# Subtracting the maximum in both softmaxes of a two-way attention read ahead of a gated FFN

## The chip, the core and the metric

One core of a Trainium2 chip runs the kernel. The metric is the device time of one execution in microseconds (us). TensorE is called PE (its weight loads PEld), VectorE DVE, ScalarE ACT, GpSimd POOL, and the sync engine, which issues most DMAs, SP.

## What is computed

```python
B, H, S, Ns, D = 8, 8, 512, 32, 64           # x: (B,H,S,D), state: (B,H,Ns,D)
scores = x @ state.T / sqrt(D)                # per batch and head, S x Ns
a = exp(scores - scores.max(-1)); a /= a.sum(-1) + 1e-9
xread = a @ state
scores2 = state @ x.T / sqrt(D)               # Ns x S
a2 = exp(scores2 - scores2.max(-1)); a2 /= a2.sum(-1) + 1e-9
sread = a2 @ x
y = concat([xread, sread], axis=2)            # heads side by side: (B*544, 512)
out = (sigmoid(y @ w_gate) * (y @ w_val)) @ w_out     # 512 -> 1536 -> 512
```

The first softmax runs over the 32 states of a token ("over states"), the second over the 512 tokens of a state ("over tokens"). Inputs and output are float32; matmuls take bfloat16.

## The kernel before

A batch is one of the eight values of B. Its 512 tokens are handled in four chunks c (token 4p + c on partition p), its 8 heads in four pairs j (e is the head within a pair).

- `load_x`, `cast_x` (L70, L88) bring x of a batch into `xf` and cast it to `xb`. `xT`, with head pairs on the partitions, comes by PE transposes for batches 0 and 1 (`xT_mm`, `xT_cp`) and by DMA transposes on SP from batch 2 on (`at_xT_dma`, L110).
- `S_mm(b, i)` (L115) makes the scores of half the head pairs in one PSUM bank, `S_exp` (L123) takes the exponential from PSUM into `E1` with no maximum subtracted. One exponential serves both softmaxes.
- Over states: `n_sum` (L137) sums over states and takes the reciprocal, `n_mul` (L169) multiplies into `ab`; `aT`, its transpose, comes by PE (batches 0 and 1) or by DMA on SP (`aT_dma`, L192).
- Over tokens: `at_Eb` (L129) casts `E1` to bfloat16 on POOL; `n_tok` and `n_split` (L143, L161; `p_tok` on POOL for batch 1) add the four chunks and split the sum into two bfloat16 terms; `sr_mm` (L201) multiplies a matrix of ones with them (L210: column sums) and `xb` with `Eb` (L213); `sr_inv` and `sr_fin` (L216, L220) divide and put the result into `XS`.
- The read over states is never formed: `sw_visit` and `sw_wide` (L239, L255) make state times w_gate and w_val for a batch in PSUM by 64x32 matmuls (L236), `sw_cp` copies it to `SW`. `gv_mm(b, f)` (L280) then makes gate and value of 128 of the 1536 channels from `SW` and `aT`: four matmuls of 128x128 by 512. `gv_th` (ACT, tanh for the sigmoid) and `gv_glu` (DVE) give `glu`. `out_mm(b, k)` (L310) makes a third of an output chunk with four matmuls; every third call ends in `res` on ACT (L323) and a DMA on SP. A ninth pass, b = 8, does the FFN of all state rows from `XS`.

Each engine runs its instructions in the order in which the code issues them; nothing is reordered. Two parts fix that order: a hand-written list from L392 to L652, which loads, brings up batches 0 and 1 and starts batch 2 (the fill), and a loop from L654 on, with twelve slots f per batch: in slot f, `out_mm(b - 1, f)`, then `gv_mm(b, f)` with tanh and glu (slots 0 and 6: `sw_wide` of the next batch first, then gv, then out), and beside it a share of the next batch's attention. `warm` (L349) issues matmuls whose result is not used.

PSUM has eight banks in four pools: `p_gv` (GV, 2), `p_out` (OU, 1), `p_sw` (SWP, 4), `p_at` (AT, 1). `sw_wide` takes all but GV: its first two tiles lie in OU and AT. A tile's bank is free when its last reader is done.

Of the kernel before, what the change touches and what calls it, by code (L numbers as in the profile page):

```python
# [16 lines left out]
def kernel(  # L17
# [70 lines left out]
    def cast_x(b, cp, lo, n):  # L88
        if b not in xbs:
            xbs[b] = xp.tile((128, 4, H, D), BF, name="xb")  # L90
        cp(xbs[b].rearrange("p c h d -> p h c d")[:, lo:lo + n], xfs[b][:, lo:lo + n])  # L91
# [31 lines left out]
    def S_exp(b, i):  # L123
        if b not in E1s:
            E1s[b] = ap_.tile((128, 4, 2, 4, Ns), FP, name="E1")
        nc.scalar.activation(E1s[b][:, :, :, 2 * i:2 * i + 2].rearrange("p c e j n -> p (c e) j n"),  # L126
                             held["S", b, i].rearrange("p c e j n -> p (c e) j n"), AF.Exp, scale=scale)

    def at_Eb(b):  # L129
        Ebs[b] = ap_.tile((128, 4, 2, 4, Ns), BF, name="Eb")  # L130
        for c in range(4):
            nc.gpsimd.tensor_copy(Ebs[b][:, c], E1s[b][:, c])  # L132
# [9 lines left out]

    def n_tok(b, e):  # L143

        if e == 0:
            held["E4", b] = ap_.tile((128, 2, 4, Ns), FP, name="E4")
        nc.vector.tensor_reduce(held["E4", b][:, e].rearrange("p j n -> p (j n)"),  # L147
                                E1s[b][:, :, e].rearrange("p c j n -> p (j n) c"), AX.X, ALU.add)

    def p_tok(b):  # L150

        E4, E5 = (ap_.tile((128, 2, 4, Ns), FP, name=f"P{i}", bufs=1) for i in range(2))
        add = nc.gpsimd.tensor_tensor
        add(E4, E1s[b][:, 0], E1s[b][:, 1], ALU.add)
        add(E5, E1s[b][:, 2], E1s[b][:, 3], ALU.add)
        add(E4, E4, E5, ALU.add)
        Es[b] = ap_.tile((128, 2, 2, 4, Ns), BF, name="Es")
        pool(Es[b][:, 0], E4)
        add(Es[b][:, 1], E4, Es[b][:, 0], ALU.subtract)

    def n_split(b, k):  # L161

        if k == 0:
            Es[b] = ap_.tile((128, 2, 2, 4, Ns), BF, name="Es")
            nc.vector.tensor_copy(Es[b][:, 0], held["E4", b])
        else:
            nc.vector.tensor_tensor(Es[b][:, 1], held["E4", b], Es[b][:, 0], ALU.subtract)
# [28 lines left out]
    def sr_parts(b):  # L196
        ps = held["sr", b]
        return (ps[:, 0:256].rearrange("p (j e n) -> p j e n", j=4, e=2),
                ps[:, 256:384].rearrange("p (j n) -> p j n", j=4))

    def sr_mm(b, place):  # L201
        Eb = Ebs[b]
        held["sr", b] = place[0].tile((128, 512), FP, name="srp", tag=place[1])
        sr, sm = sr_parts(b)
        if b in Es:
            terms = [(e, Es[b][:, k, e]) for e in range(2) for k in range(2)]
        else:
            terms = [(e, Eb[:, c, e]) for e in range(2) for c in range(4)]
        for i, (e, rhs) in enumerate(terms):
            nc.tensor.matmul(sm, ones[:, e], rhs, start=(i == 0), stop=(i == len(terms) - 1))  # L210
        for j in range(4):
            for c in range(4):
                nc.tensor.matmul(sr[:, j], xbs[b][:, c, 2 * j:2 * j + 2].rearrange("p h d -> p (h d)"),  # L213
                                 Eb[:, c, :, j], start=(c == 0), stop=(c == 3))

    def sr_inv(b):  # L216
        r2 = held["r2", b] = ap_.tile((128, 4, Ns), FP, name="r2")
        nc.vector.reciprocal(r2, sr_parts(b)[1])  # L218

    def sr_fin(b):  # L220
        if ("r2", b) not in held:
            sr_inv(b)
        sr, r2 = sr_parts(b)[0], held["r2", b]
        for e in range(2):
            rows = slice(e * 64, (e + 1) * 64)
            nc.vector.tensor_tensor(XS[rows, :, b * Ns:(b + 1) * Ns], sr[rows, :, e], r2[rows], ALU.mult)
# [166 lines left out]
    load_x(0, nc.sync, 4)  # L393
    load_x(1, nc.sync, 4)
# [4 lines left out]
    nc.vector.memset(sTz, 0.0)  # L399
    ident_e = ident.rearrange("p (g e u) -> p e g u", e=2, u=8)  # L400
    pre = wp.tile((128, 2), FP, name="pre")
    nc.scalar.activation(pre[:, 0:1], ones[:, 0, 0:1], AF.Exp)

    cast_x(0, pool, 0, 2)
    warm(12, OU)
    cast_x(0, vec, 2, 2)
    warm(16, GV)
    warm(8, OU)
    cast_s(0, pool)
    load_w(1, 256, 256)  # L410
# [24 lines left out]
    load_w(1, 0, 256)
    cast_x(1, act, 0, 2)
    S_mm(0, 0, AT, (1,))
    S_exp(0, 1)
    cast_x(1, vec, 4, 2)
    n_sum(0, 1)  # L440
    load_w(0, 512, 512)
    S_exp(0, 0)
    xT_mm(1, 0, SWP)
    xT_mm(1, 1, SWP)
    cast_x(1, pool, 6, 2)
    at_Eb(0)
    xT_mm(1, 2, AT)
    xT_cp(1, 2, vec)
    n_sum(0, 0)
    xT_mm(1, 3, OU)  # L450
    xT_cp(1, 3, act)
    S_mm(1, 1, GV)
    load_sb(2)
    xT_cp(1, 0, act)
    S_exp(1, 1)
    xT_cp(1, 1, vec)
    S_mm(1, 0, AT)
    n_mul(0, 1, nc.vector)
    n_mul(0, 0, nc.vector)
    n_sum(1, 1)  # L460
    sw_visit(0, 256, 256)
    sr_mm(0, OU)
    S_exp(1, 0)
    sw_cp(0, 256, 2, 1, act)
    aT_mm(0, AT)
    sw_visit(1, 256, 256)
    sw_cp(0, 256, 2, 0, act)
    aT_cp(0, 0, act)
    n_sum(1, 0)
    sw_visit(1, 0, 256)  # L470
    aT_cp(0, 1, vec)
    load_w(0, 1024, 512)
    load_w(1, 512, 512)
    load_w(1, 1024, 512)
    n_mul(1, 1, nc.gpsimd)
    sr_fin(0)
# [72 lines left out]
    sw_cp(1, 1024, 1, 0, vec)
    gv_glu(1, 1)  # L550
    cast_x(2, act, 0, 4)
    cast_x(2, pool, 4, 4)
    sw_visit(0, 512, 512, 1)
    gv_mm(1, 11, SWP)
    gv_glu(1, 6)
    sw_cp(0, 512, 1, 0, vec)
    gv_mm(0, 11, GV)
    gv_th(1, 11)
    sw_cp(0, 512, 1, 1, vec)
    at_xT_dma(2)  # L560
    gv_glu(1, 11)
    gv_mm(0, 6, SWP)
    gv_mm(0, 9, SWP)
    gv_th(0, 11)
    gv_th(0, 6)
    gv_glu(0, 11)
    gv_mm(0, 10, GV)
    gv_glu(0, 6)
    gv_th(0, 9)
    gv_mm(0, 7, SWP)  # L570
    gv_glu(0, 9)
    gv_mm(0, 5, SWP)
    gv_th(0, 10)
    gv_th(0, 7)
    gv_th(0, 5)
    load_wo(1)
    gv_glu(0, 7)
    gv_glu(0, 10)
    gv_mm(1, 4, SWP)
    gv_th(1, 4)  # L580
    gv_glu(0, 5)
    gv_mm(0, 4, GV)
    gv_mm(1, 8, SWP)
    gv_glu(1, 4)
    gv_mm(0, 8, SWP)
    sr_fin(1)
    gv_th(1, 8)
    pad(2, 6)
    out_mm(0, 0, AT)
    gate(glus[1][:, 4, 0:1])  # L590
    load_wo(2)
    load_x(3, nc.gpsimd)
    gv_th(0, 4)
    gv_mm(1, 9, SWP)
    gv_th(0, 8)
    gv_glu(1, 8)
# [141 lines left out]
```

## Time and profile before

| | |
|---|---|
| Time, median of 3 runs | 225.48 us (225.43 to 225.87) |
| The profiled execution | 226.03 us, of which the span of its instructions is 224.2 us |
| PE, DVE, ACT, POOL busy | 217.0, 140.7, 127.6, 48.8 us |
| First gate matmul (L288) starts | 16.40 us |
| First `sw_wide` of the loop starts | 56.22 us |
| One steady batch of the loop | 23.6 us |
| DMA | 27.37 MB, mean 122 GB/s |

Times in the profile count from the span's start. A row of the timeline gives start, duration, engine, line and operation, output<-input with partitions x elements, the count where several are merged, and in brackets how long the engine was idle before and what ended that. A PE duration includes the time to drain, so the step to the next matmul is shorter than it. The chain of work is followed back from the last instruction to whatever released each one.

### The profile page before, as it was taken

The page shows a single profiled execution, that of the slowest core. Times are in us where ns is not written, and L with a number is a line of the kernel's source. Part 1 is how long each engine was busy: PE and PEld are TensorE (multiplying, and loading weights), DVE is VectorE, ACT ScalarE, POOL GpSimd, SP SyncE. Part 2 cuts the span into 40 slices and gives each one's busy share as a digit, 9 for nine tenths or more (in the row PEclk, how much of TensorE's full clock was granted, in tenths as well). Part 3 has the DMA queues.
Part 4 walks back from the last instruction along what each step waited for, and adds up shares of the span by engine and source line. Part 5 has one row for each costly group of instructions (what it writes and reads, how often), then busy time and mean ns, then how long its engine had stood idle before and what let it go on. Part 6 is the DMA issues. An engine that isn't in the chain of part 4 may idle for free.

```text
span 224.2 us, 4791 instructions
## 1 busy us (share of the span) xinstructions
PE 217.0 (97%) x1859; PEld 111.2 (50%) x1859; DVE 140.7 (63%) x248; ACT 127.6 (57%) x239; POOL 48.8 (22%) x85
## 2 busy tenths in 40 slices
PE   7789999999999999999999999999999999999994
PEld 6654444444444545454444454454445444466744
DVE  3599897779368756885488648864787434422311
ACT  2587885645676557656675667556755444423311
POOL 3799560362041004200240006000200000000001
PEclk9999999999999999999999999999999999999999
DMA  6999989753898352627362521253122111111114
GB/s 188 289 201 206 280 130 179 114 193 78 147 292 274 71 151 76 219 59 126 100 225 50 121 96 61 44 81 117 47 78 66 50 50 47 67 73 48 50 26 114
DMA packets 38566, 27.37 MB, mean 122 GB/s; under 512 B 21168, under 2 KB 33840, under 8 KB 38544
## 3 DMA queue, kind: packets, MB, share of 16 engines
q1 hardware_dynamic: 31392, 19.74, 32.5%
q0 software_dynamic: 6864, 7.14, 17.6%
q8 instruction: 14, 0.23, 0.4%
q10 hardware_dynamic: 288, 0.20, 0.3%
q14 instruction: 8, 0.07, 0.1%
HBM read 18.35 MB, written 8.91 MB: 122 GB/s over the span
## 4 chain that ended last, share of the span: by engine, by line
PE 91%; DVE 3%; DMA 2%; ACT 1%; SPq 1%; issue 0%
PE outp L319 38%; PE gvp L288 37%; PE swp L236 5%; PE gvp L291 5%; DMA xf<-in_x_dram 2%; PE srp L213 1%; PE Sp L121 1%; PE outp L339 1%; DVE rs L139 1%; PE srp L210 1%; SPq L74 1%; DVE ab L173 1%; DVE ri L141 0%; DVE r L218 0%; PE xTp L105 0%; PE warm L353 0%
## 5 line engine op out<-in xcount | busy, mean ns | idle before, releaser
L303 DVE SCALAR_TENSOR_TENSOR glu<-th,gvp 128x512 bf16<-128x512 f32 (+1 forms) x108 | 69.9, 655 | 64.0 <-ACT th L298 48.7
L319 PE MATMUL outp<-wo,glu 128*128 128x512 bf16 x396 | 98.2, 379 | 0.0
L288 PE MATMUL gvp<-aT,SW 128*128 128x512 bf16 x384 | 96.3, 379 | 0.3 <-DVE aT L190 0.2
L298 ACT ACTIVATE th<-gvp 128x512 f32<-128x512 f32 (+1 forms) x108 | 61.8, 574 | 60.6 <-PE gvp L288 49.2
L288 PEld LDWEIGHTS <-SW 128*128 128x128 bf16 x384 | 36.3, 98 | 44.7 <-issue 3.1
L319 PEld LDWEIGHTS <-glu 128*128 128x128 bf16 x396 | 37.4, 98 | 40.8 <-issue 0.4
L274 ACT CAST SW<-swp 128x512 bf16<-128x512 f32 x70 | 38.8, 586 | 4.7 <-PE swp L236 3.3
L132 POOL CAST Eb<-E 128x256 bf16<-128x256 f32 x32 | 11.5, 407 | 89.9 <-ACT E L126 89.9
L323 ACT ACTIVATE res<-outp 128x512 f32<-128x512 f32 x33 | 19.7, 597 | 17.6 <-PE outp L319 17.6
L274 DVE CAST SW<-swp 128x512 bf16<-128x512 f32 x26 | 17.1, 683 | 1.6 <-PE swp L236 1.4
L91 POOL CAST xb<-xf 128x1024 bf16<-128x1024 f32 (+1 forms) x13 | 13.8, 1093 | 12.1 <-DMA xf<-in_x_dram 10.7
L330 POOL DMA_DIRECT2D out_dram<-res x2 | 1.1, 542 | 60.0 <-ACT res L323 60.0
L147 DVE TENSOR_REDUCE E<-E 128x128 f32<-128x512 f32 x12 | 12.4, 1035 | 0.0
L139 DVE TENSOR_REDUCE rs<-E 128x16 f32<-128x512 f32 x16 | 10.8, 676 | 1.3 <-ACT E L126 1.3
L126 ACT ACTIVATE E<-Sp 128x512 f32<-128x512 f32 x16 | 9.6, 604 | 2.4 <-PE Sp L121 2.4
L173 DVE TENSOR_TENSOR ab<-E,ri 128x512 bf16<-128x512 f32 x12 | 9.6, 804 | 0.0
L236 PE MATMUL swp<-wg,sTc 64*32 64x512 bf16 (+1 forms) x192 | 8.4, 328 | 0.0
L236 PEld LDWEIGHTS <-sTc 64*32 64x32 bf16 x384 | 4.5, 91 | 7.4 <-issue 4.7
L218 DVE RECIPROCAL r<-srp 128x128 f32<-128x128 f32 x8 | 7.6, 950 | 0.0
L121 PEld LDWEIGHTS <-xT 128*128 128x128 bf16 x128 | 5.5, 98 | 4.0 <-DVE xT L108 1.0
L236 PE MATMUL swp<-wv,sTc 64*32 64x512 bf16 (+1 forms) x192 | 7.4, 322 | 0.0
L291 PE MATMUL gvp<-XS,wg 128*128 128x256 bf16 x48 | 7.2, 273 | 0.0
(64 smaller groups left out, 122.0 us busy)
## 6 DMA issues: line engine op xcount, KB each, us to landing
out_dram<-res SPq DMA_DIRECT2D x31, 256.0 KB, 2.6
xf<-in_x_dram SPq DMA_DIRECT2D x12, 256.0 KB, 4.5
xf<-in_x_dram SPq DMA_DIRECT2D x3, 1024.0 KB, 6.8
wo<-in_moe_w_out_dram POOLq DMA_DIRECT2D x3, 512.0 KB, 5.9
wg<-in_moe_w_gate_dram POOLq DMA_DIRECT2D x2, 512.0 KB, 9.2
wv<-in_moe_w_val_dram POOLq DMA_DIRECT2D x2, 512.0 KB, 10.8
xf<-in_x_dram POOLq DMA_DIRECT2D x2, 512.0 KB, 10.4
xf<-in_x_dram POOLq DMA_DIRECT2D x1, 1024.0 KB, 9.2
```

The source lines that it names most:

```text
L91: cp(xbs[b].rearrange("p c h d -> p h c d")[:, lo:lo + n], xfs[b][:, lo:lo + n])
L139: nc.vector.tensor_reduce(rs, halfE(b, i), AX.X, ALU.add)
L147: nc.vector.tensor_reduce(held["E4", b][:, e].rearrange("p j n -> p (j n)"), E1s[b][:, :, e].rearrange("p c j n -> p (j n) c"), AX.X, ALU.add)
L173: eng.tensor_tensor(abs_[b].rearrange("p c e (j n) -> p (c e) j n", n=Ns)[:, ce, 2 * i:2 * i + 2], halfE(b, i)[:, ce], ri[:, ce].unsqueeze ...
L236: nc.tensor.matmul(pss[e][j * Ns:(j + 1) * Ns, o:o + n], sTc[rows, b, j] if b > 1 else sTz[rows, b, j, e], (wg, wv)[w][rows, j, lo:lo + n] ...
L274: cp(*sw_left.pop((b, lo, w, e)))
L288: nc.tensor.matmul(ps, SWs[b][:, g, w, fs], aTs[b][:, :, g], start=(g == 0), stop=(g == 1))
L291: nc.tensor.matmul(ps, (wg, wv)[w][:, j, fs], XS[:, j], start=(j == 0), stop=(j == 3))
L298: nc.scalar.activation(th, held["gv", b, f][0], AF.Tanh, scale=0.5)
L303: nc.vector.scalar_tensor_tensor(glus[b][:, f], held["th", b, f], 1.0, held["gv", b, f][1], ALU.add, ALU.mult)
L319: nc.tensor.matmul(ops[b, c], glus[b][:, f, c * 128:(c + 1) * 128], wo[:, f], start=(f == 0), stop=(f == NF - 1))
L323: nc.scalar.activation(res, ops[b, c], AF.Copy, scale=0.5)
```

## The change

Over states: `S_max` takes the maximum of each token and head over its 32 scores on DVE, from PSUM; `S_sub` subtracts it, PSUM to `E1`; `S_exp` runs in place on `E1`.

Over tokens: `cT_mm` makes the scores once more, transposed (states on the partitions, tokens along the row, 32 states by 4 pairs per bank), `cT_max` their maximum and its scaled negative, `cT_exp` the exponential with that as bias and the sum as a second output, `cT_nrm` the reciprocal (DVE) and the product in bfloat16 (POOL), `c_dma` transposes the two rows back by DMA on SP. `sr_mm` has no sums left, and `sr_cp`, one half on ACT and one on DVE, copies its result. `at_Eb`, `n_tok`, `p_tok`, `n_split`, `sr_inv` and `sr_fin` are gone.

The fill is written anew: batch 1 is loaded and brought up ahead of batch 0, and the transposed scores of batches 0 and 1 are made in the loop's pass of batch 7. `xb` and `xT` of batches 0 and 1 have buffers of their own until then; `xb` of the others has three. In the loop `cast_x` and `at_xT_dma` stand in slot 1 instead of 5, and `n_mul` runs on POOL.

```diff
@@ functions
-    def S_exp(b, i):
-        nc.scalar.activation(E1s[b][...], held["S", b, i], AF.Exp, scale=scale)
+    def S_max(b, i):
+        mx = held["mx", b, i] = ap_.tile((128, 8, 2), FP, name="mx")
+        nc.vector.tensor_reduce(mx, ps, AX.X, ALU.max)
+    def S_sub(b, i):
+        nc.vector.tensor_tensor(halfE(b, i), ps, mx.unsqueeze(3).to_broadcast((128, 8, 2, Ns)), ALU.subtract)
+    def S_exp(b, i):
+        nc.scalar.activation(halfE(b, i), halfE(b, i), AF.Exp, scale=scale)
-    def at_Eb(b): / n_tok / p_tok / n_split / sr_parts / sr_inv / sr_fin
+    def cT_mm(b, places):
+        pss = [p[0].tile((128, 512), FP, name="cTp", tag=p[1]) for p in places]
+        for j in range(4):
+            for e in range(2):
+                rows = slice(e * 64, (e + 1) * 64)
+                nc.tensor.matmul(pss[e][j * Ns:(j + 1) * Ns], sTz[rows, b, j, e],
+                                 xTs[b][rows, j].rearrange("p c t -> p (c t)"), start=True, stop=True)
+    def cT_max(b, e):
+        nc.vector.tensor_reduce(mx, held["cT", b][e], AX.X, ALU.max)
+        nc.vector.tensor_scalar(nb, mx, -scale, None, op0=ALU.mult)
+    def cT_exp(b, e):
+        nc.scalar.activation(ex, held["cT", b][e], AF.Exp, bias=held["nb", b, e], scale=scale, accum_out=cs)
+    def cT_nrm(b, e, eng):
+        nc.vector.reciprocal(rc, held["cs", b, e])
+        eng.tensor_scalar(held["cN", b][:, e], held["cE", b, e], rc, None, op0=ALU.mult)
+    def c_dma(b):
+        for e in range(2):
+            nc.sync.dma_start_transpose(Ebs[b][:, :, e], held["cN", b][:, e])
     def sr_mm(b, place):
-        for i, (e, rhs) in enumerate(terms):
-            nc.tensor.matmul(sm, ones[:, e], rhs, ...)
         for j in range(4):
             for c in range(4):
                 nc.tensor.matmul(sr[:, j], xbs[b][:, c, 2 * j:2 * j + 2]..., Eb[:, c, :, j], ...)
+    def sr_cp(b, e, cp):
+        cp(XS[rows, :, b * Ns:(b + 1) * Ns], held["sr", b][rows, :, e])
@@ the fill, up to the first gate matmul (in part)
+    load_x(1, nc.sync, 4)
...
+    load_x(0, nc.sync, 4)
...
+    cast_x(0, vec, 0, 2)
+    S_mm(1, 0, SWP)
+    xT_cp(1, 2, vec)
+    S_max(1, 0)
...
+    n_sum(1, 1)
...
+    S_max(0, 0)
+    sw_visit(1, 256, 256)
...
+    S_sub(0, 0)
+    S_max(0, 1)
+    S_exp(0, 0)
+    n_mul(1, 1, nc.gpsimd)
+    aT_mm(1, GV)
+    aT_cp(1, 0, act)
...
+    sw_visit(1, 512, 512, 1)
+    S_sub(0, 1)
+    S_exp(0, 1)
+    sw_visit(0, 512, 512, 1)
...
+    warm(15, GV)
...
+    aT_cp(1, 1, vec)
+    gv_mm(1, 3, GV)
@@ the loop, b = 3 to 6 (batch 2 one slot later; nb = b + 1)
+    slot 0: S_mm(nb, 0, AT)
+    slot 1: S_max(nb, 0); S_mm(nb, 1, SWP); cast_x, at_xT_dma of nb + 1
+    slot 2: S_sub(nb, 0); S_max(nb, 1)
+    slot 3: S_exp(nb, 0); S_sub(nb, 1); sr_mm(b, AT)
+    slot 4: sr_cp(b) on act and vec; n_sum, n_mul(nb, 0); S_exp(nb, 1)
+    slot 5: n_sum, n_mul(nb, 1)            slot 6: aT_dma(nb)
+    slot 7: cT_mm(nb, (AT, SWP))           slot 8: cT_max(nb, 0)
+    slot 9: cT_exp(nb, 0); cT_max(nb, 1)   slot 10: cT_exp(nb, 1); cT_nrm(nb, 0)
+    slot 11: cT_nrm(nb, 1); c_dma(nb)
+    b = 7: the same five steps of cT for batch 0 in slots 0 to 4 and for batch 1 in 3 to 7,
+           sr_mm and sr_cp of batch 0 in slot 8 and of batch 1 in slot 11
```

The loop's part is written here as a table of slots; the sw_cp on ACT stay where they were (slots 0, 1, 3, 4 and 6, 7, 9, 10).

More of the change, by code (lines that the diff above doesn't have):

```diff
@@ L194, in aT_dma @@
             nc.sync.dma_start_transpose(aT_tile(b)[:, c], abs_[b][:, c].rearrange("p e k -> p (e k)"))
[L196 to L199, printed above, removed]
-    def sr_mm(b, place):
[L202 to L208, printed above, removed]
-        for i, (e, rhs) in enumerate(terms):
-            nc.tensor.matmul(sm, ones[:, e], rhs, start=(i == 0), stop=(i == len(terms) - 1))
+    def cT_mm(b, places):
[5 more added lines that the diff above has]
+                                 xTs[b][rows, j].rearrange("p c t -> p (c t)"), start=True, stop=True)
+        held["cT", b] = pss
@@ L214, in sr_mm @@
                                  Eb[:, c, :, j], start=(c == 0), stop=(c == 3))
[L216 to L226, printed above, removed]
+    def sr_cp(b, e, cp):
+        rows = slice(e * 64, (e + 1) * 64)
+        cp(XS[rows, :, b * Ns:(b + 1) * Ns], held["sr", b][rows, :, e])
     sw_left = {}
@@ L458 @@
[L458 to L464, printed above, removed]
+    load_x(0, nc.sync, 4)
+    cast_x(1, pool, 0, 2)
+    xT_mm(1, 0, SWP)
+    xT_cp(1, 0, vec)
+    load_w(1, 256, 256)
+    xT_mm(1, 1, AT)
+    load_sb(1)
+    load_w(0, 256, 256)
+    sT_pad(0, 0, act)
+    load_w(1, 512, 512)
+    cast_x(1, act, 4, 2)
+    xT_cp(1, 1, act)
+    xT_mm(1, 2, GV)
+    cast_x(1, pool, 6, 2)
+    cast_x(0, vec, 0, 2)
@@ new lines @@
+    S_mm(1, 0, SWP)
+    xT_cp(1, 2, vec)
+    S_max(1, 0)
+    xT_mm(0, 0, AT)
+    xT_mm(1, 3, SWP)
+    cast_x(0, act, 2, 2)
+    xT_mm(0, 1, GV)
+    xT_cp(0, 0, act)
+    xT_cp(1, 3, act)
+    warm(3, OU)
+    load_w(0, 0, 256)
+    S_sub(1, 0)
+    xT_cp(0, 1, act)
+    cast_x(0, act, 4, 2)
+    S_mm(0, 0, GV, (0,))
+    S_mm(1, 1, SWP)
+    S_exp(1, 0)
+    cast_x(0, vec, 6, 2)
+    warm(3, AT)
+    xT_mm(0, 3, GV)
+    xT_mm(0, 2, SWP)
+    S_max(1, 1)
+    xT_cp(0, 2, act)
+    load_sb(3)
@@ new lines @@
+    load_w(1, 0, 256)
+    warm(6, OU)
+    S_sub(1, 1)
+    load_sb(2)
+    load_w(0, 512, 512)
+    S_mm(0, 0, AT, (1,))
+    warm(12, SWP)
+    n_sum(1, 0)
+    S_exp(1, 1)
+    S_mm(0, 1, AT, (0,))
+    sT_mm(1, SWP)
+    xT_cp(0, 3, act)
+    S_mm(0, 1, OU, (1,))
+    n_mul(1, 0, nc.gpsimd)
+    sw_visit(0, 256, 256)
+    n_sum(1, 1)
+    sT_cp(1, act)
+    sw_cp(0, 256, 2, 0, act)
+    warm(8, GV)
+    S_max(0, 0)
+    sw_visit(1, 256, 256)
+    sw_cp(1, 256, 2, 0, act)
+    sw_cp(0, 256, 2, 1, vec)
@@ new lines @@
+    gv_th(0, 9)
+    gv_glu(0, 9)
+    gv_th(0, 11)
+    gv_th(0, 8)
+    load_wo(2)
+    S_max(2, 0)
+    S_sub(2, 0)
+    S_exp(2, 0)
+    S_mm(2, 1, GV)
+    out_mm(0, 6, AT)
+    load_x(3, nc.gpsimd)
+    cast_x(3, pool, 4, 4)
+    out_mm(0, 2)
+    sw_cp(2, 0, 0, 1, act)
+    gv_glu(0, 8)
+    gv_glu(0, 11)
+    sw_cp(2, 0, 1, 0, act)
+    cT_mm(2, (SWP, SWP))
+    sw_visit(1, 1024, 512, 0)
+    n_sum(2, 0)
+    out_mm(0, 8)
+    n_mul(2, 0, nc.vector)
+    sw_cp(2, 0, 2, 1, act)
+    sw_cp(2, 0, 1, 1, act)
@@ new lines @@
+    S_max(2, 1)
+    S_sub(2, 1)
+    sw_cp(2, 0, 2, 0, act)
+    sw_cp(2, 0, 0, 0, act)
+    S_exp(2, 1)
+    cT_max(2, 0)
+    sw_cp(1, 1024, 0, 0, act)
+    out_mm(0, 7, GV)
+    gate(xTs[2][:, 0, 3, 0:1])
+    cT_max(2, 1)
+    cast_x(3, pool, 0, 4)
+    cT_exp(2, 0)
+    n_sum(2, 1)
+    n_mul(2, 1, nc.vector)
+    aT_dma(2)
+    cT_exp(2, 1)
+    cT_nrm(2, 1, nc.gpsimd)
+    out_mm(0, 10)
+    gv_mm(1, 7, SWP)
+    out_mm(0, 9)
+    gv_th(1, 7)
+    sw_cp(1, 1024, 0, 1, vec)
+    sw_wide(2, 1)
@@ L563 @@
[L563 to L589, printed above, removed]
@@ L654, with row @@
+    def row(b, f):
+        if f == 0:
+            S_mm(b, 0, AT)
+        elif f == 1:
+            S_max(b, 0)
+            S_mm(b, 1, SWP)
+        elif f == 2:
+            S_sub(b, 0)
+            S_max(b, 1)
+        elif f == 3:
+            S_exp(b, 0)
+            S_sub(b, 1)
+        elif f == 4:
+            n_sum(b, 0)
+            n_mul(b, 0, nc.gpsimd)
+            S_exp(b, 1)
+        elif f == 5:
+            n_sum(b, 1)
+            n_mul(b, 1, nc.gpsimd)
     for b in range(2, B + 1):
```

409 lines of the change are left out of this document (166 added, 243 removed).

## Prediction

> **What bounds the kernel now.** I read the first page first: busy time by engine and the span in 40 slices.
>
> ```profile
> PE 217.0 (97%) x1859; PEld 111.2 (50%) x1859; DVE 140.7 (63%) x248; ACT 127.6 (57%) x239; POOL 48.8 (22%) x85
> ...
> PE   7789999999999999999999999999999999999994
> ```
>
> PE is busy in every slice but the first few, so a busy share alone cannot tell a bound from a queue of slow matmuls. The chain of work that ended last can.
>
> ```profile
> PE 91%; DVE 3%; DMA 2%; ACT 1%; SPq 1%; issue 0%
> ```
>
> The chain is PE almost everywhere; DVE, ACT and DMA stand in it only before 18 us. Next the table by stretches. A steady batch takes 23.6 us and PE has no gap in it, while DVE has 7.0 us free and ACT 8.7.
>
> ```profile
> 103.50:127.10 23.60, 23.60 (x197) 11.11 (x196) 16.58 (x27) 14.94 (x29) 3.87 (x6) 1.00 0.49 124
> ```
>
> The columns are the stretch, then busy us of PE, PEld, DVE, ACT and POOL, the granted clock (1.00) and DMA. So the time is the start of the first gate matmul (L288, 16.40 us), plus all PE work behind it, plus waits, and almost none are there today. I price the change in these three terms. The profiled execution took 226.03 us around a span of 224.2; the runs' median is 225.48, so I add the difference in span to 225.48.
>
> **Term 1, PE work.** Three stretches of the timeline give prices (start, us, engine, line).
>
> ```profile
> 22.13 1.04 PE L288 MATMUL gvp<-aT,SW 128*128 128x512 bf16 x4
> ...
> 23.10 0.41 PE L236 MATMUL swp<-wg,sTz 64*32 64x512 bf16 x8
> ...
> 23.44 1.90 PE L288 MATMUL gvp<-aT,SW 128*128 128x512 bf16 x8
> ```
>
> Four gate matmuls step by 0.863 us in the chain; here they take 0.97 until the eight 64x32 matmuls start, and those 0.34. A lone group of eight costs 0.97 + 0.34 - 0.863 = 0.45 us. The new cT_mm has that very form (eight of 64x32 by 512), so 0.45 each where it stands alone. Between like groups it is 0.22 (138.84 to 139.06 below).
>
> [...]
>
> ```profile
> 146.53 0.39 PE L210 MATMUL srp<-Es,ones 128*128 128x128 bf16 x4
> 146.76 0.63 PE L213 MATMUL srp<-Eb,xb 128*128 128x64 bf16 x16
> 147.22 1.03 PE L319 MATMUL outp<-wo,glu 128*128 128x512 bf16 x4
> ```
>
> sr_mm is 0.69 a batch: 0.23 for the four L210 sums, which go, and 0.46 for L213, which stays.
>
> From the loop's first wide visit (56.22 in the trace) to the end, before has sr_mm for batches 3 to 7, 5 x 0.69 = 3.45. After has all but nothing of it in the fill: eight sr_mm, 8 x 0.46 = 3.68 (batch 2 slips into the loop, batches 0 and 1 into the last batch), and cT_mm for 3 to 7, 0 and 1, 7 x 0.45 = 3.15. Difference **+3.4**. From the first gate matmul to the loop before needs 56.22 - 16.40 = 39.8. After drops two sr_mm (-1.4), has the weight visits in fewer, joined groups (about -0.9 by the 0.45 and 0.22 above), gains cT_mm(2) beside a visit (+0.2): 37.7. Difference **-2.1**.
>
> **Term 2, the first gate matmul.** Before:
>
> ```profile
> 10.38 0.62 POOL L91 CAST xb<-xf 128x512 bf16<-128x512 f32 x1 [1.22 <-DMA xf<-in_x_dram]
> ...
> 16.40 1.02 PE L288 MATMUL gvp<-aT,SW 128*128 128x512 bf16 x4 [0.18 <-DVE aT L190]
> ```
>
> The eight quarter loads land up to 10.33; the fourth had landed by 7.5, so about 0.71 apart. After, batch 1 is loaded first and is first through. I walk DVE, in its order of instructions, with steps between neighbours in the trace (0.63 to 0.71 for a 128x512 reduction, 0.64 for a product of that size, 0.38 for a cast). S_max and S_sub are not in the trace; their nearest rows are the reduction L139 (0.68) and a PSUM copy L274 (0.68). Bounds 0.4 and 1.05 (L147): over the eight before the gate matmul that is -2 to +3 us, and I take 0.65. DVE casts batch 0's first quarter (lands 8.2), copies xT, S_max(1,0) at 9.0, S_sub 9.7, casts batch 0's last quarter 10.4, S_max(1,1) 10.95, S_sub 11.6, n_sum(1,0) 12.25 when ACT's exponential is done, n_sum(1,1) 13.25, then, queued ahead of the copy that the gate matmul needs: S_max(0,0), a weight copy, S_sub(0,0), S_max(0,1), S_sub(0,1), and aT_cp(1,1) at 17.3 to 17.7. ACT's aT_cp(1,0) sits behind S_exp(0,0) and ends near 17.5. POOL's two products (1.06 each) end at 15.4. On PE 15 warm matmuls (about 1.0) stand behind visits that want the 512-wide w_val load, issued near 7.05 and by the row of such loads (9.9 us) here near 16.9: 18.5. Between 17.7 and 18.5 I take 18.0: **+1.6**.
>
> **Term 3, waits.** Behind it gv(1,2) waits for ACT's queue of weight copies (the copy of the (0,0,256) visit near 20.7) and gv(1,1) for glu(1,3), which stands behind two n_sum and two weight copies on DVE: 0.7. Later bank waits in the fill, 0.6. Together **+1.3** (0 to 3).
>
> In the loop a slot of 1.73 us has 0.86 of gate matmul and 0.86 of output matmul. DVE fits: its fullest slot (glu, S_sub, S_max) is 2.0 us, but sr_mm lengthens the next. The tight place is ACT ahead of a wide visit, which takes the out bank:
>
> ```profile
> 137.88 1.03 PE L288 MATMUL gvp<-aT,SW 128*128 128x512 bf16 x4
> ...
> 138.08 0.60 ACT L323 ACTIVATE res<-outp 128x512 f32<-128x512 f32 x1 [0.22 <-PE outp L319]
> 138.57 0.59 ACT L298 ACTIVATE th<-gvp 128x512 f32<-128x512 f32 x1
> ...
> 138.84 0.41 PE L236 MATMUL swp<-wg,sTc 64*32 64x512 bf16 x8
> 139.06 0.40 PE L236 MATMUL swp<-wv,sTc 64*32 64x512 bf16 x8
> ```
>
> res ends 0.80 behind gv's start and the visit begins at 0.96: 0.16 of room. After, slot 4 gives ACT th, a weight copy, sr_cp and the second S_exp. From gv's start: th 0.63, copy 1.13, sr_cp 1.61, S_exp 1.86, res 2.37 to 2.97, where the visit is due at 1.73 + 0.96 = 2.69: it waits 0.3, in batches 3 to 6: 1.2. Slot 10 has cT_exp in place of that: res ends at 2.71 to 2.9, a wait of 0.08, 0.33 for batch 2 with sr_cp: 0.65. sr_mm in slot 3 takes the bank that S_sub reads until 2.61 and is due at 2.59: 0.07 x 6 = 0.4. The last sr_cp before gv(8,0): 0.15. Together **+2.4** (0.2 to 4; cT_exp writes a sum too, no row shows that, and I take S_exp's 0.60, at most twice that).
>
> At nothing: the casts of scores and token sums that go (hidden on POOL and DVE under a dense PE); cT_nrm on POOL (0.61 for a cast, 1.06 for a product, in a queue 16% busy per batch); two more SP transposes a batch (1.27 each, 2.5 to land): issued in slot 11, they land about 2 us ahead of sr_mm. Cover gone, each us late is a us of PE.
>
> Sum: 3.4 - 2.1 + 1.6 + 1.3 + 2.4 = 6.6; 225.48 + 6.6 = **232.1**, by the profiled execution 232.6. Own range 230 to 234.
>
> POOL's products beside DVE: at 44.30 to 46.35 POOL ran two while two glu stepped by 0.61, unslowed. [...]
>
> **Rivals.** (a) No bank waits in the loop: ACT's steps are shorter or the room greater. For it: ACT has 8.7 us free a batch. Against: 0.16 of room. 232.1 - 2.3 = 229.8. Chance 0.2. (b) A longer fill: batch 0's last quarter or the w_val load 1.2 us late, then twice that through glu's backlog: 234.5 to 235.5. Chance 0.13. (c) Transposed rows late: DVE, POOL and SP in a row behind aT and xT transposes (SP's 4 take 5 us); each us past the 2 of room is paid six times, so 1 us is 238. Chance 0.08. (d) Not slower: DVE's order matters less than I think and batch 1, alone at the front, has its aT by 13.5 (its S_mm can run at 7.5, then six DVE steps and two POOL products); the gate matmul then starts near 14 and with no waits the time is 225.5 - 2.4 + 1.3 = 224.4. It decides at a start of 15.1 without waits. Against: DVE runs in order and waits for batch 0's quarters. Chance 0.03. (e) That the new softmax isn't what runs: the order of instructions has the 16 maxima, 16 differences, 64 matmuls and 16 transposes, so no time is given to it.
>
> **How the numbers follow.** Forecast 0.56, (a) 0.2, (b) 0.13, (c) 0.08, (d) 0.03. From 228.8 (below (a) by its unknowns) to 236 some 0.88 is held; the unmeasured steps ask for it. Within 0.2%, what a measurement of this kernel can tell, lies only the upper edge of (d): faster 0.03, same 0.01, slower 0.96.
>
> **What would show it.** First gate matmul near 18 us; first wide visit of the loop near 57; batch stretch 24.2 to 24.4 instead of 23.6; a wide visit beginning about 1.25 behind the start of gv in slot 5; sr_mm 0.46, cT_mm 0.45. A batch at 23.9 means (a); sr_mm waiting on a DMA means (c); a first gate matmul before 15.1 means (d). A DVE reduction from PSUM far from 0.68 would move terms 2 and 3 together.

## The result and the profile after

| | before | after |
|---|---|---|
| Time, median of 4 runs each, on one chip | 225.60 us (225.43 to 225.87) | 235.69 us (235.38 to 236.14) |
| Ratio | | 1.0447, 95% interval 1.0426 to 1.0469 |
| The profiled execution and its span | 226.03, 224.2 us | 235.38, 233.5 us |
| First gate matmul | 16.40 us | 17.73 us (forecast 18.0) |
| First `sw_wide` of the loop | 56.22 us | 56.47 us (forecast about 57) |
| From there to the first gate matmul over `XS` | 139.75 us | 148.78 us |
| From there to the end | 28.3 us | 28.3 us |

The kernel became 10.1 us slower by the medians; 6.6 were forecast. By the two profiled executions, which the account below follows, the span grew by 9.3. The fill came out as forecast or a little better. The loop did not: it grew by 9.03 us where 5.8 were forecast (3.4 of PE work and 2.4 of waits). So 3.2 us of loop are missing from the sum.

The page of the changed kernel, the same rows as before (line numbers of the changed kernel from here on; `gv_mm` is L283 there, `out_mm` L314, the visits L231):

```profile
PE 221.3 (95%) x1887; PEld 111.2 (48%) x1887; DVE 139.0 (60%) x267; ACT 143.3 (61%) x290; POOL 68.5 (29%) x74
...
PE   5788999999999969999999999999999999999995
...
PE 35%; ACT 6%; SPq 5%; DMA 2%; DVE 1%; issue 1%; POOL 1%; ACTq 0%
```

PE's busy time grew by 4.3 us, the span by 9.3, so about half of the loss is time in which PE stands. A 6 appears in slice 15, in the middle of the loop, where before had 9s throughout. ACT gained 15.7 us and POOL 19.7, DVE lost 1.7. The chain of work no longer runs through PE alone: ACT, SP's queue and DMAs are in it. The stretches of one steady batch and of one half (columns as before):

```profile
131.84:156.41 24.57, 24.12 (x202) 11.10 (x201) 15.50 (x29) 16.33 (x34) 7.18 (x7) 1.00 0.34 86
156.41:168.98 12.57, 12.35 (x112) 5.95 (x112) 8.01 (x14) 8.08 (x17) 2.39 (x2) 1.00 0.32 65
```

A steady batch takes 24.57 (24.2 to 24.4 forecast) and PE now has 0.45 us of gaps in it. Two waits make them, both in PE's list of waits:

```profile
PE swp L231 <- ACT res L318: 1.9, 8, 0.4
PE gvp L283 <- DMA aT<-ab: 1.8, 1, 1.8
```

(Total us, times, longest.) The first is the one forecast: wide visits wait for `res` on ACT. Here it is in slot 5, by the timeline of the changed kernel, ACT first:

```profile
142.63 0.58 ACT L269 CAST SW<-swp 128x512 bf16<-128x512 f32 x1
143.10 0.27 ACT L221 CAST XS<-srp 64x128 bf16<-64x128 f32 x1
143.25 0.64 ACT L137 ACTIVATE E<-E 128x512 f32<-128x512 f32 x1
143.79 0.58 ACT L318 ACTIVATE res<-outp 128x512 f32<-128x512 f32 x1
```

PE in the same stretch:

```profile
143.18 1.03 PE L283 MATMUL gvp<-aT,SW 128*128 128x512 bf16 x4
144.42 0.41 PE L231 MATMUL swp<-wg,sTc 64*32 64x512 bf16 x8 [0.22 <-ACT res L318]
```

The visit starts 1.25 behind the gate matmul, as the forecast said. In slot 11 it starts 1.26 behind (155.15 to 156.41), where the forecast had 1.04. The second wait was not in the sum at all. It comes once, for 1.8 us, in batch 3:

```profile
83.51 0.81 PE L283 MATMUL gvp<-aT,SW 128*128 128x512 bf16 x3 [1.82 <-DMA aT<-ab]
```

The timeline of the changed kernel before it, on POOL:

```profile
68.61 2.02 POOL L91 CAST xb<-xf 128x1024 bf16<-128x1024 f32 x2 [14.84 <-DMA xf<-in_x_dram]
70.59 1.04 POOL L152 TENSOR_TENSOR ab<-E,ri 128x512 bf16<-128x512 f32 x1
73.02 1.05 POOL L152 TENSOR_TENSOR ab<-E,ri 128x512 bf16<-128x512 f32 x1 [1.39 <-ACT th L293]
```

and on SP's queue:

```profile
58.96 2.53 SPq L209 DMA_TRANSPOSE Eb<-cN  x2
61.54 0.57 SPq L74 DMA_DIRECT2D xf<-in_x_dram  x1
...
70.65 5.13 SPq L113 DMA_TRANSPOSE xT<-xb  x4
75.88 0.52 SPq L320 DMA_DIRECT2D out_dram<-res  x1
76.51 5.77 SPq L173 DMA_TRANSPOSE aT<-ab  x4
```

POOL stood 14.84 us in front of batch 4's cast because that batch's load is issued by SP only at 61.54, behind batch 3's four and batch 2's two transposes. Both of batch 3's products stand behind the cast on POOL, and its four aT transposes stand behind batch 4's four xT transposes on SP. The last leaves SP at 82.28, and PE waits.

### The profile page after: what moved, and what is told of

The parts are those of the page before. It is cut to its first block, busy times and chain, and to the rows that moved or that the text cites. A ratio compares the mean times of both kernels' runs of the same rounds, so it can differ in the third digit from the quotient of the medians.

```text
span 233.5 us, 4978 instructions
## 1 busy us (share of the span) xinstructions
PE 221.3 (95%) x1887; PEld 111.2 (48%) x1887; DVE 139.0 (60%) x267; ACT 143.3 (61%) x290; POOL 68.5 (29%) x74
## 4 chain that ended last, share of the span: by engine, by line
PE 35%; ACT 6%; SPq 5%; DMA 2%; DVE 1%; issue 1%; POOL 1%; ACTq 0%
PE outp L314 16%; PE gvp L283 10%; PE gvp L286 5%; SPq L113 2%; SPq L173 2%; ACT SW L269 2%; ACT cE L196 1%; PE swp L231 1%; DMA xf<-in_x_dram 1%; PE outp L334 1%; PE srp L216 1%; ACT th L293 1%; ACT res L318 1%; DMA aT<-ab 1%; DVE glu L298 1%
## 5 line engine op out<-in xcount | busy, mean ns | idle before, releaser
L314 PE MATMUL outp<-wo,glu 128*128 128x512 bf16 x396 | 98.9, 379 | 0.2 <-ACT res L318 0.2
L283 PE MATMUL gvp<-aT,SW 128*128 128x512 bf16 x384 | 96.7, 379 | 2.0 <-DMA aT<-ab 1.8
L283 PEld LDWEIGHTS <-SW 128*128 128x128 bf16 x384 | 36.2, 98 | 46.8 <-issue 5.4
L314 PEld LDWEIGHTS <-glu 128*128 128x128 bf16 x396 | 36.8, 98 | 41.0 <-issue 2.6
L269 ACT CAST SW<-swp 128x512 bf16<-128x512 f32 x74 | 41.1, 587 | 3.5 <-PE swp L231 3.2
L204 POOL TENSOR_SCALAR cN<-cE,rc 128x512 bf16<-128x512 f32 x16 | 25.0, 1563 | 52.4 <-DVE rc L201 44.5
L318 ACT ACTIVATE res<-outp 128x512 f32<-128x512 f32 x33 | 19.7, 596 | 17.3 <-PE outp L314 17.2
L152 POOL TENSOR_TENSOR ab<-E,ri 128x512 bf16<-128x512 f32 x14 | 14.6, 1047 | 42.7 <-ACT th L293 28.0
L91 POOL CAST xb<-xf 128x1024 bf16<-128x1024 f32 (+1 forms) x13 | 12.4, 975 | 28.6 <-DMA xf<-in_x_dram 28.5
L269 DVE CAST SW<-swp 128x512 bf16<-128x512 f32 x22 | 14.7, 680 | 3.2 <-PE swp L231 3.2
L196 ACT ACTIVATE cE<-cTp,nb 128x512 f32<-128x512 f32 x16 | 11.1, 696 | 0.7 <-DVE nb L190 0.5
L129 DVE TENSOR_REDUCE mx<-Sp 128x16 f32<-128x512 f32 x16 | 10.9, 680 | 0.4 <-PE Sp L121 0.4
L134 DVE TENSOR_TENSOR E<-Sp,mx 128x512 f32<-128x512 f32 x16 | 11.0, 686 | 0.2
L188 DVE TENSOR_REDUCE cm<-cTp 128x1 f32<-128x512 f32 x16 | 10.9, 684 | 0.0
L137 ACT ACTIVATE E<-E 128x512 f32<-128x512 f32 x16 | 10.2, 639 | 0.5 <-DVE E L134 0.5
L231 PE MATMUL swp<-wg,sTc 64*32 64x512 bf16 (+1 forms) x192 | 8.5, 327 | 1.9 <-ACT res L318 1.9
L231 PEld LDWEIGHTS <-sTc 64*32 64x32 bf16 x384 | 5.5, 91 | 8.9 <-issue 6.9
## 6 DMA issues: line engine op xcount, KB each, us to landing
wg<-in_moe_w_gate_dram POOLq DMA_DIRECT2D x2, 512.0 KB, 10.1
```

The source lines that it names most:

```text
L152: eng.tensor_tensor(abs_[b].rearrange("p c e (j n) -> p (c e) j n", n=Ns)[:, ce, 2 * i:2 * i + 2], halfE(b, i)[:, ce], ri[:, ce].unsqueeze ...
L196: nc.scalar.activation(ex, held["cT", b][e], AF.Exp, bias=held["nb", b, e], scale=scale, accum_out=cs)
L204: eng.tensor_scalar(held["cN", b][:, e], held["cE", b, e], rc, None, op0=ALU.mult)
L231: nc.tensor.matmul(pss[e][j * Ns:(j + 1) * Ns, o:o + n], sTc[rows, b, j] if b > 1 else sTz[rows, b, j, e], (wg, wv)[w][rows, j, lo:lo + n] ...
L269: cp(*sw_left.pop((b, lo, w, e)))
L283: nc.tensor.matmul(ps, SWs[b][:, g, w, fs], aTs[b][:, :, g], start=(g == 0), stop=(g == 1))
```

## The experiments

Theory: the loop loses what PE has to do more, plus ACT's waits ahead of wide visits, plus this one late load. Rivals: DMA transposes are late in general, other engines (DVE with its maxima above all) hold the loop, or PE's extra work is hidden. The table gives, for each kernel, the median, the median of before beside it on the same chip, and stretches of its profiled execution, from wide visit to wide visit: the half with slots 0 to 5 in batch 3 and in batches 4 to 6, the half with slots 6 to 11 in batches 3 to 5, and the last stretch, from batch 7's second visit (in slot 6 of batch 6) to the first gate matmul over `XS`. The medians are over all executions of a kernel, and some of these have a mean granted clock of 0.991 to 0.993, of which the last section tells (batch 3's half in e2, e4 and e9 holds 3.4 us of half clock); so the other stretches, and not the medians, decide between the theories.

| kernel | time | before | slots 0-5, batch 3 | slots 0-5, 4 to 6 | slots 6-11 | last |
|---|---|---|---|---|---|---|
| before | | | 11.70 | 11.71 | 11.93 | 33.49 |
| changed | 235.69 | 225.60 | 14.45 | 12.58 | 11.98 | 36.27 |
| e1_load4 | 234.96 | 225.24 | 12.58 | 12.58 | 11.98 | 36.27 |
| e2_exp_late | 236.59 | 225.24 | 15.62 | 12.29 | 12.26 | 36.54 |
| e3_dve_sum | 235.79 | 225.24 | 12.74 | 12.58 | 11.90, in batch 3 12.17 | 36.96 |
| e4_twice_cT | 237.84 | 225.24 | 15.95 | 12.58 | 12.20 | 36.92 |
| e5_load4_mid | 234.03 | 225.45 | 12.58 | 12.58 | 11.98 | 36.27 |
| e6_sums_late | 234.55 | 225.45 | 13.77 | 12.29 | 11.98 | 36.27 |
| e8_no_colmax | 234.48 | 225.45 | 13.74 | 12.58 | 11.83 | 35.90 |
| e9_join_cT | 235.76 | 225.37 | 15.94 | 12.59 | 11.98 | 36.05 |
| e10_three | 232.70 | 225.37 | 12.97 | 12.29 | 11.98 | 36.04 |
| e11_copy_only | 236.03 | 225.37 | 14.38 | 12.58 | 11.98 | 36.44 |
| e12_no_rowmax_look (one run) | 240.98 | 225.37 | 14.93 | 13.77 | 12.00 | 36.29 |

### The load of batch 4

```diff
+    load_x(4, nc.sync)
     at_xT_dma(3)
...
     c_dma(2)
-    load_x(4, nc.sync)
```

> The load of batch 4's x is issued on SP ahead of batch 3's transposes instead of behind them. My theory: batch 3's rows aT came 1.85 us late once, because POOL's cast of batch 4 waited 14.8 us for that load and batch 3's two products stood behind it on POOL. Then the gate matmul at 83.5 waits for nothing, and the time falls by 1.7 to 1.9 us, to about 233.8. Rival: the transposes are late because SP and the DMA queues are full of transposes in that stretch, whatever POOL does; then the wait stays above 1 us and the time moves by less than 0.6.

Batch 3's half fell to 12.58, by 1.87 (1.7 to 1.9 foreseen), and the wait for aT is gone. But the half before it grew from 11.80 to 13.28, and the time fell by no more than 0.4 us against before (9.7 slower instead of 10.1). The scores of batch 3 now wait for xT:

```profile
62.06 0.20 PE L121 MATMUL Sp<-sTz,xT 128*128 128x64 bf16 x1
62.55 0.20 PE L121 MATMUL Sp<-sTz,xT 128*128 128x64 bf16 x1 [0.29 <-DMA xT<-xb]
63.04 0.20 PE L121 MATMUL Sp<-sTz,xT 128*128 128x64 bf16 x1 [0.28 <-DMA xT<-xb]
63.60 0.32 PE L121 MATMUL Sp<-sTz,xT 128*128 128x64 bf16 x5 [0.35 <-DMA xT<-xb]
```

The 1 MB load now moves beside those transposes; they took SP 6.03 us instead of 5.17. Cause and place were right, the cure moved the wait. So the load went between the two groups of transposes:

```diff
     at_xT_dma(3)
...
+    load_x(4, nc.sync)
     c_dma(2)
-    load_x(4, nc.sync)
```

> The load of batch 4's x is issued on SP between batch 3's xT transposes and batch 2's cN transposes (in the changed kernel: behind both; in the run before this one: ahead of both, which removed batch 3's wait of 1.85 us but made S_mm(3) wait for xT, and its half batch 1.48 us longer). My theory: the load landed too late for POOL, and put ahead of the xT transposes it shares the DMA engines with them; between the two, neither waits, and from the first gate matmul to the end the profiled execution is 1.7 to 1.9 us shorter than the changed kernel's 215.8, some 214.0. Rival: the load then holds up the cN transposes or still runs into aT's, and under 0.6 us is gained.

Neither wait is left; every other stretch of the table is as in the changed kernel to 0.01 us. From the first gate matmul to the end it took 214.3 us against 215.8, and the time is 8.6 us above before instead of 10.1. The batch after the load shows what was cured:

```profile
66.41 2.02 POOL L91 CAST xb<-xf 128x1024 bf16<-128x1024 f32 x2 [12.11 <-DMA xf<-in_x_dram]
71.01 1.05 POOL L152 TENSOR_TENSOR ab<-E,ri 128x512 bf16<-128x512 f32 x1 [2.58 <-DVE ri L146]
```

The product waits for its reciprocal again and not for the cast. The rival, that transposes are late in general, falls.

The size of this wait is not fixed by the order of issue alone. In the changed kernel PE waits 1.82; in e8, e6 and e9, with the load in the same place, it waits 1.10, 1.42 and 1.62. In e3 the loop starts later (57.85 against 56.47), SP issues the load at 62.28, 4.43 us behind the loop's first wide visit instead of 5.07, and PE stands 0.11 ahead of the first gate matmul that needs aT (at 83.10). So the 12.74 of e3 in batch 3 is no gain of its edit: there the load came in time.

### ACT ahead of the wide visits

```diff
         elif f == 4:
...
-            S_exp(b, 1)
         elif f == 5:
+            S_exp(b, 1)
```

> The second exponential of the row part is issued one slot later, behind res. My theory: in slot 5 it stood between two others on ACT and made res, and so the wide visit, 0.28 us late in batches 3 to 6. Then the first half of a batch takes about 12.3 us instead of 12.58, the visit starts 0.96 to 1.0 behind the gate matmul's start, and the time falls by about 1.1, to 234.6. Rival: the visit waits for something beside ACT (or the exponential only moves its 0.64 us to the next slot's copies); then the time stays within 0.3 of 235.7.

The half with slot 5 fell by 0.29 as foreseen and the visit starts 0.96 behind the gate matmul. The other half grew by 0.28: nothing was gained. The gate matmul behind the visit now stands in its middle, its four matmuls spread over 1.31 us instead of 1.04, and DVE shows why:

```profile
144.59 0.29 DVE L221 CAST XS<-srp 64x128 bf16<-64x128 f32 x1
144.92 0.69 DVE L144 TENSOR_REDUCE rs<-E 128x16 f32<-128x512 f32 x1
145.71 0.25 DVE L146 RECIPROCAL ri<-rs 128x16 f32<-128x16 f32 x1
146.00 0.69 DVE L298 SCALAR_TENSOR_TENSOR glu<-th,gvp 128x512 bf16<-128x512 f32 x1
```

`glu(5)`, whose end frees a gate bank, comes behind `sr_cp` and the first sum: a second wait had been standing right behind ACT's. With that sum moved too:

```diff
         elif f == 4:
+            pass
-            n_sum(b, 0)
-            n_mul(b, 0, nc.gpsimd)
-            S_exp(b, 1)
         elif f == 5:
+            n_sum(b, 0)
+            n_mul(b, 0, nc.gpsimd)
+            S_exp(b, 1)
```

> The second exponential of the row part and the first of its two sums (with its product) come one slot later. Moving the exponential alone took the 0.29 us from the half batch with slot 5 and put 0.28 on the next half, where the gate matmul waited for glu(5) behind sr_cp and that sum on DVE. My theory: DVE's queue is the second wait behind ACT's, and with both moved the halves take 12.29 and 11.98: 0.29 less a batch in batches 3 to 6, 1.1 to 1.4 us in all. Rival: a third wait of like size stands behind these (the rows aT, now issued later on POOL, or the gate matmul's banks again), and the halves still sum to 24.5.

12.29 and 11.98, as foreseen; the time is 9.1 above before; in its profiled execution the wait for aT, which the edit does not aim at, is 0.4 shorter too (1.42 for 1.82). The next edit asks what slot 11's 1.26 is made of:

```diff
-        nc.scalar.activation(ex, held["cT", b][e], AF.Exp, bias=held["nb", b, e], scale=scale, accum_out=cs)
+        nc.scalar.activation(ex, held["cT", b][e], AF.Exp, bias=held["nb", b, e], scale=scale)
...
+        nc.vector.tensor_reduce(held["cs", b, e], held["cE", b, e], AX.X, ALU.add)
```

> The exponential over tokens no longer forms its sum; DVE sums the row afterwards, ahead of the reciprocal (16 reductions of 128x512 more on DVE, each about 0.68 us). My theory: the sum's separate 0.21 us on ACT, and a slower exponential, set slot 11's visit 1.26 behind the gate matmul; without it 1.04, so five times 0.2, about 1.1 less: 234.6. Rival: DVE's 1.4 us a batch more comes ahead of a glu that the output matmuls wait for, and the time grows by up to 3 us.

The halves with slot 11 in batches 4 and 5 fell by 0.08, not 0.2, and the visit starts 1.17 behind. (In batch 3 the half grew to 12.17: its visit waits for a glu on DVE.) The changed kernel's accumulator instruction lasts 0.21 us, but the one behind it starts 0.10 after it (155.65 and 155.75), so at most 0.10 of it is paid. In the last batch DVE's added sums cost 0.77 (a gate matmul waits 0.84 for a glu), so the exchange does not pay. The other part of slot 11 came out with the column maximum left out:

```diff
     def cT_max(b, e):
...
-        nc.vector.tensor_reduce(mx, held["cT", b][e], AX.X, ALU.max)
-        nb = held["nb", b, e] = ap_.tile((128, 1), FP, name="nb")
-        nc.vector.tensor_scalar(nb, mx, -scale, None, op0=ALU.mult)
+        pass
...
-        nc.scalar.activation(ex, held["cT", b][e], AF.Exp, bias=held["nb", b, e], scale=scale, accum_out=cs)
+        nc.scalar.activation(ex, held["cT", b][e], AF.Exp, scale=scale, accum_out=cs)
```

> cT_max is left out in all batches, so the softmax over tokens does not subtract its maximum (no bias in its exponential). My theory: DVE's 0.84 us for each of the 16 is hidden under PE but for the last batch, where a gate matmul waits 0.35 us for a glu behind it: 0.2 to 0.5 us less, 235.2 to 235.5, so the column part's price is its matmuls on PE and its two ACT steps, not its maximum. Rival: the exponential's longer step (0.58 us against 0.49 for tanh) comes from the bias, and without it each batch gains 0.1 to 0.2 more: 1.0 to 1.5 us less.

The rival was right: 0.15 less behind every slot 11 (two exponentials) and another 0.22 in the last batch, where `cT_max` had held up a glu. The time is 9.0 above before; in the profiled execution the wait for aT is again shorter, by 0.7. The groups by form, of the changed kernel and of this one (count, then busy us and mean ns):

```profile
L196 ACT ACTIVATE cE<-cTp,nb 128x512 f32<-128x512 f32 x16 | 11.1, 696 | 0.7 <-DVE nb L190 0.5
...
L196 ACT ACTIVATION_READ_ACCUMULATOR cE<-cTp,nb 128x1 f32 x16 | 3.3, 208 | 0.0
```

Without the maximum:

```profile
L193 ACT ACTIVATE cE<-cTp 128x512 f32<-128x512 f32 x16 | 9.7, 608 | 0.0
```

With its bias held in a tile the exponential was 88 ns longer, 696 against 608, sixteen of each. At the visit behind slot 11, e8 gained 0.15 and e3 0.08; the two were not tried together, but their sum fits the 0.22 by which that wait was missed.

### PE's work

```diff
-        for j in range(4):
+        for j in (0, 1, 2, 3, 0, 1, 2, 3):
```

> The eight matmuls of each transposed score tile are issued twice over, with the same result (this work is doubled). My theory: PE is the bound wherever cT_mm stands in the loop, so every us of PE work is paid in full: seven groups in the loop times 0.22 us, and up to 0.22 for the one in the fill, 1.5 to 1.8 more: about 237.4. Rival: part of PE's growth hides in its waits for ACT and DVE, and the time grows by under 0.8.

Every half with a cT_mm grew by 0.22 (11.98 to 12.20), the last stretch by 0.65 for its three, the fill by 0.21: 1.7 in all, of the 1.5 to 1.8 foreseen. PE's work in the loop is paid in full, and the rival falls. The median is 12.6 above before; the rest of that is in batch 3 and is told under the hardware below.

```diff
                 for k in range(2):
-                    if 0 <= f - 3 * k < 5:
+                    if f == 3 * k == 0 or 0 < f - 3 * k < 5:
                         col(k, f - 3 * k)
+                    if f == k == 0:
+                        cT_mm(1, (SWP, SWP))
```

> Only the last batch's two cT_mm are joined. Theory: a lone group of eight 64x32 matmuls costs 0.45, one behind another of its form 0.22, so the last batch (first output matmul of batch 7 to the first gate matmul over XS) is 0.23 shorter, and the time by as much, which is at the edge of what the runs can tell. Rival: the price is in the matmuls and not in the change of form; then the stretch stays as it is.

The last stretch fell by 0.22 or 0.23, here and in the next kernel, as the change of form has it; the time itself, 10.4 above before, cannot tell so little.

### The maximum over rows

```diff
     def S_max(b, i):
...
-        nc.vector.tensor_reduce(mx, ps, AX.X, ALU.max)
+        pass
...
     def S_sub(b, i):
...
-        nc.vector.tensor_tensor(halfE(b, i), ps, mx.unsqueeze(3).to_broadcast((128, 8, 2, Ns)), ALU.subtract)
+        pass
...
     def S_exp(b, i):
-        nc.scalar.activation(halfE(b, i), halfE(b, i), AF.Exp, scale=scale)
+        nc.scalar.activation(halfE(b, i), held["S", b, i].rearrange("p c e j n -> p (c e) j n"), AF.Exp, scale=scale)
```

> S_max and S_sub are left out in all batches, so the row softmax does not subtract its maximum; its exponential reads the scores in PSUM. This tells what the maximum over rows costs. My theory: in the fill it is DVE's queue of these reductions that sets the first gate matmul, so it starts at 14.5 to 16 us instead of 17.7; in the loop they cost what sr_mm waits for its bank (0.12 a batch), and the visits wait for ACT as before: together 2.5 to 4 us less, 231.7 to 233.2. Rival: the first gate matmul is set by the weight loads and PE's own queue (start above 17), and less than 1.5 us is gained.

It took 240.65 us (median of six; five of them 239.96 to 242.83) beside 225.45: with less work, 5 us more than the changed kernel. The sixth execution, the profiled one, took 580.71 us; in its first 240 us, four gate matmuls in a row lasted 2.41 to 2.65 us, 1.03 in the changed kernel. Nothing here explains that, and no stretch of it is used. Another profiled execution of the same kernel tells where the 5 us go:

> The same kernel as the one without S_max and S_sub, whose profiled execution was disturbed; its time of 240.65 was not foreseen (231.7 to 233.2 were). New theory: the score bank, which S_sub on DVE freed in slot 2, is now held until ACT's exponential in slots 3 and 4, so sr_mm in slot 3 waits for it, 0.6 to 1 us in each of six batches, and more through what stands behind it: sr_mm waits 4 us or more in all and the halves with slots 0 to 5 take 13.2 or more. Rival: S_exp from PSUM is itself much longer than 0.64, or the fill grew.

```profile
142.21 1.03 PE L280 MATMUL gvp<-aT,SW 128*128 128x512 bf16 x4
144.47 0.63 PE L213 MATMUL srp<-Eb,xb 128*128 128x64 bf16 x16 [1.23 <-ACT E L134]
```

`sr_mm` waits 1.23 us in each of four batches for the exponential that now frees its bank, and the halves with slots 0 to 5 take 13.77. In the changed kernel `S_sub`, a DVE operation one slot earlier, frees it, and `sr_mm` comes 0.98 behind the gate matmul where 0.86 would be without any wait. So the expectation had mistaken what `S_sub` does besides subtracting. The clean version leaves only the maximum out:

```diff
     def S_max(b, i):
...
-        nc.vector.tensor_reduce(mx, ps, AX.X, ALU.max)
+        pass
...
     def S_sub(b, i):
...
-        nc.vector.tensor_tensor(halfE(b, i), ps, mx.unsqueeze(3).to_broadcast((128, 8, 2, Ns)), ALU.subtract)
+        nc.vector.tensor_copy(halfE(b, i), held["S", b, i].rearrange("p c e j n -> p (c e) j n"))
```

> S_max is left out in all batches and S_sub only copies the scores out of PSUM, so the row softmax does not subtract its maximum, but the bank is freed by DVE as in the changed kernel. Theory: DVE's queue ahead of the first gate matmul is 2.7 us shorter, but w_val lands at 16.0 to 16.5 and 15 warm matmuls stand behind it on PE, so the first gate matmul comes at 17.1 to 17.9, no more than 0.5 earlier; in the loop sr_mm no longer waits for its bank, 0.12 a batch; together 0.3 to 1.2 us less. Rival: DVE alone set the first gate matmul; it starts at 15 to 16, and 2.3 to 3.3 us are gained.

No stretch of the loop moved by more than 0.2 and the time is 10.7 above before: 16 reductions of 0.68 us on DVE, 10.9 us of work, cost nothing that can be measured. Even `sr_mm`'s 0.12 stayed, since the copy stands behind `glu(2)`, which waits for its tanh. In the fill DVE stood 1.08 us ahead of its copy to aT, until ACT's copy of the other half had ended, and the first gate matmul still came at 18.07; the rival's 15 to 16 falls. So DVE's queue was not what held it alone: ACT's copy and PE's own visits and warm matmuls end there too.

### Three edits together

> Three edits together: batch 4's load between the transposes, the exponential and the sums of the row part one slot later, and the two cT_mm of the last batch issued one behind the other. If what they remove adds up: 1.87 (batch 3's wait), 4 to 5 times 0.29, and 0.23 for one change of tile form less in the last batch, 3.3 us less than the changed kernel: 232.2 to 232.6. If batch 3's rows come late again because the products stand one slot later on POOL, 1 us more.

The load between the transposes, the later row part and the joined groups give 232.70 us, 7.3 above before (ratio 1.0332, 1.0309 to 1.0355) against 10.1. The gains add up, except in batch 3, whose half stays 0.7 longer than the others: its products, a slot later, bring aT 0.6 us late once more. No version here comes near the kernel before.

## Why the prediction was right or wrong

- **Sign and mechanism** were right: PE bound, more PE work in the loop, ACT late ahead of wide visits. The size was 3.6 us short by the medians: 235.69 lies above the own range of 230 to 234, and inside the wider 228.8 to 236 only near its edge. Rival (b) named the nearest time, 234.5 to 235.5, but from a longer fill, and the fill grew by 0.25 us.
- **Term 1** held: a lone cT_mm steps by 0.95 + 0.35 - 0.863 = 0.44 (147.80, 148.75, 149.10), sr_mm by 0.46, and the doubled and the joined groups show that both the 0.22 and the change of form are paid.
- **Term 2** came out at +1.33 for +1.6. The walk put DVE's copy to aT at 17.3 at the earliest and it ran at 17.25. So close a fit is partly luck: in the profiled executions of nine other kernels with the same code up to there (e1 to e6, e8 to e10) the first gate matmul began at 17.40 to 19.06. That DVE alone sets the start is not so, by the copy-only kernel. The fill from there fell by 1.08; -2.1 and +1.3 had been forecast.
- **Term 3, slot 5**: 0.3 forecast, 0.28 to 0.29 shown by moving the exponential. That a removed wait would be gained is another matter: the wait for glu right behind it took 0.28 back.
- **Term 3, slot 11**, was mis-sized: cT_exp was taken at S_exp's 0.60, "at most twice that". It is 0.70 and a read of the accumulator: the visit is 0.30 late where 0.08 was taken, 0.22 more behind each of batches 3 to 5, and the output matmul at 180.97 waits in the same way behind batch 6: 0.9 us. Behind batch 2 it is 0.43 where 0.33 was taken.
- **The step that failed** is the sentence "at nothing". It weighed the two added transposes by their own landing (they are early: SP issues batch 6's until 160.58, sr_mm needs them at 164.68) and left out what they are put in front of: the load of batch 4, in the hand-written list. The load's lateness goes through POOL's cast to both products and to aT: 1.87 us, once, in this execution. Rival (c) had the row of POOL, SP and aT right, but as a steady loss.
- These two steps (1.87, and 0.9 with 0.1 for batch 2) and 0.3 in small waits make up the 3.2 but for 0.1. The small ones: sr_mm waits 0.12 for its bank in four batches, where 0.07 in six was taken, and 0.22 stands in the last batch behind cT_max.
- cT_nrm on POOL lasts 1.56 us where at most 1.06 was assumed; it cost nothing, since its rows land early.

## What to carry to other kernels

Where an edit adds an instruction to a queue, list all that stands behind it in that queue, loads of later batches above all, and follow each to its last reader; weighing only the added instruction's own result misses this. A wait that one engine ends can have a second one right behind it: look at what the next instruction would wait for before counting the gain. And an operation that looks superfluous may be the one that frees a bank early.

## What the runs showed of the hardware that was not expected

- **A short stop of PE was followed, in some executions, by half its clock.** In the changed kernel's profiled execution PE stood 1.82 us in batch 3 and went on at full clock. In that of the kernel with joined groups it stood 1.62 at the same place, and went on at half. Stretches of both (third column from the end: granted clock):

```profile
84.00:86.00 2.00, 2.00 (x18) 1.05 (x17) 1.17 (x2) 0.60 (x1) 1.77 (x2) 1.00 0.91 225
86.00:88.00 2.00, 2.00 (x18) 1.01 (x17) 0.52 (x2) 1.03 (x2) 0.00 (x0) 1.00 0.65 131
```

With joined groups:

```profile
84.00:86.00 2.00, 2.00 (x5) 0.69 (x6) 0.10 (x1) 0.60 (x1) 2.00 (x3) 0.52 1.05 304
86.00:88.00 2.00, 1.95 (x13) 0.98 (x13) 1.19 (x2) 0.00 (x0) 0.45 (x1) 0.63 0.52 93
```

  The four gate matmuls behind the stop step by 1.61 us in all (83.98 to 85.59) instead of 0.86 (83.51 to 84.37); the half took 15.94 instead of 14.45. Where the load came late (the changed kernel, e2, e3, e4, e6, e8, e9, e11), 15 of 45 executions had a mean clock of 0.991 to 0.993, and 1 of 7 of e7 and e12; where the load was moved (e1, e5, e10) and PE stood there 0.6 us at most in the profiled executions, none of 17. That is why e4's median is higher than its matmuls explain: its three executions with full clock took 236.06 to 236.98, the others 238.71 to 239.58.

  In the three profiled executions with the drop (e2, e4, e9) PE had stood 1.61, 1.64 and 1.62 us, and the granted clock is half for 3.40 us in each, by stretches of 2 us (in e9 1.92 and 1.48 of the two above). The changed kernel stood 1.82 and the copy-only kernel 1.75 at the same place, both with a wait of 0.36 or 0.37 ahead of the wide visit before it as in those three, and went on at full clock. So the length of the stop does not decide by itself; what does is not shown, and no run here moved a stop on purpose to test it.

- **A product with one number per partition took longer on POOL**: 1563 ns for 128x512 where a product of two tiles took 1047.

```profile
L204 POOL TENSOR_SCALAR cN<-cE,rc 128x512 bf16<-128x512 f32 x16 | 25.0, 1563 | 52.4 <-DVE rc L201 44.5
...
L152 POOL TENSOR_TENSOR ab<-E,ri 128x512 bf16<-128x512 f32 x14 | 14.6, 1047 | 42.7 <-ACT th L293 28.0
```
